# State products of two head pairs moved to the array's other two corners, their sums in a second PSUM bank, first MLP's weights loaded to match

## The chip, the cores and the metric

One core of a Trainium2 chip. The metric is the device time of one execution in microseconds (us); smaller is better. Times are medians of several executions; the profile is one execution, taken by the hardware profiler. Engines are called PE (TensorE matmul), PEld (its weight loads), DVE (VectorE), ACT (ScalarE), POOL (GpSimd) and SP (SyncE, which here only issues DMAs).

## The reference

Attention with decay ("retention") over 2 batches, 8 heads, 768 tokens and 64 channels a head, then two MLPs over the 1536 tokens with 512 channels and 2048 hidden units.

```python
for b in range(nb):                       # blocks of the sequence
    intra = (q_b @ k_b.T * Dmask) @ v_b
    inter = (q_b * lam_pow) @ kv_state
    out[b] = intra + inter
    kv_state = lam_block * kv_state + (k_b * rev_pow).T @ v_b
x = out as (1536, 512)
x = leaky(x @ w_in) @ w_out               # first MLP, slope alpha per hidden unit
x = relu(x @ w2_in)**2 @ w2_out           # second MLP
```

Everything is float32; the weights arrive as 64-bit numbers and are converted on the chip.

## The kernel before

**Retention.** The kernel takes blocks of 128 tokens. Step n of 12 is block c = n // 2 of batch b = n % 2, so the two batches alternate, and the state that step n needs was made by step n - 2. The heads form four pairs a = 0 to 3; of a pair, head t = 0 has its 64 channels in partitions 0 to 63 and head t = 1 in 64 to 127. One step of the main loop is, on PE in this order:

- `outputs(n)`: 8 products of masked scores and v (L1035; stationary 128 x 64), and for c > 0 on top of them, in the same PSUM tile, 8 products of state and q (L1043). The state product of head t uses rows 64t to 64t + 63 of the array and writes to partitions 64t to 64t + 63. So it uses two of the array's four 64 x 64 corners, (0, 0) and (1, 1).
- `products(n)`, called at the end of `outputs(n)` for c < 5: 8 products of the decayed k (called r) and v (L1058), which give the state's increment pk.
- `scores(n + 3)`: 8 products of k and q (L998).

A product in float32 is two PE instructions, so 8 products stand as x16 in the trace.

The order on the other engines is the order in which the loop issues. In step n DVE multiplies the scores of step n + 2 by the decay mask (`decay`, L1010), adds the state (`keep_state`, L1084) and, for the steps without a second copy, takes the rest of the output (`keep_rest`, L1078). ACT copies the output to the first MLP's input in a reduced type (`keep_output`, L1068), makes a second copy `whole` in steps 3, 5, 7 and 9 (L1071) and makes the decayed old state (L1090). POOL makes the factors of step n + 2 (`factors`: q times growth, L1017, then r times fade, L1020) and for steps 3, 5, 7 and 9 the rest of the output from `whole` (L1078). SP issues the loads: k and q of step n + 4 (L897, L898), v and r of step n + 2 (L903, L907), and in eight of the steps one 512 KB piece of the first MLP's weights (`load_piece`, L173). Between these, DVE and ACT convert weight pieces (`Conversion`: L185 and L188 on ACT, L194 and L200 on DVE, the cast L210 on ACT, the rest L216 on DVE); piece number 3 begins in step 9 with L194.

PSUM has 8 banks of 2 KB a partition: four for scores (pool `psc`), two for outputs (`pso`, one bank a step, two in turn) and two for pk (`psk`).

**First MLP.** When the loop is done, PE computes three hidden blocks (`first`, L297, 12 matmuls each) before the first sums (`second`, L358). Step s = 0 to 11 of this stage activates the hidden block on ACT and DVE (L311, L313, L319), splits it into two parts (`cast`, L330 on ACT; `rest`, L338 on DVE), and `second(0)` needs both parts of the block s = 0: its third matmul is the first to read the second part. The remaining hidden units of this MLP and the second MLP follow as Strassen products (L630, L784, L837); their weights are loaded by SP (L391), two 512 KB loads a piece, and converted (L402 on ACT is the first operation on a loaded piece).

The channels of x stand in four blocks of 128 partitions, one for each head pair.

Of the kernel before, what the change touches and what calls it, by code (L numbers as in the profile page):

```python
# [127 lines left out]
def retention_then_two_mlps(  # L128
# [36 lines left out]
    raws, bits, weights = {}, {}, {}  # L165
    loaded = []

    def load_piece(queue=nc.scalar):
        if len(loaded) < len(SEQ):
            j = SEQ[len(loaded)]  # L170
            raws[j] = mem.claim(LOW, RAW + 4 * (len(loaded) % 4), 4)
            loaded.append(j)
            queue.dma_start(raws[j].view(U32), w1[j])  # L173

    class Conversion:
        def __init__(self):
# [208 lines left out]
    def convert(k):  # L385

        half = k % 2
        layer, _, p = pieces[k]
        raw = yield from taken(LOW, RAW + 8 * half, 8)
        for e in range(2):  # L390
            nc.sync.dma_start(  # L391
                raw.view(U32)[:, 2 * e * DM : 2 * (e + 1) * DM],
                (w1, w2)[layer][2 * (2 * p + e) + half],
            )
        bit = yield from taken(LOW, BIT + 7 * half, 4 if half else 7)
        both = raw.view(U32, 2)
        low, high = both[:, :, 0], both[:, :, 1]
        f = bit.view(F32)[:, 0 : 2 * DM]
        x = bit.view(U32)[:, 0 : 2 * DM]
        t = yield from step(  # L400
            ACT, 1.15, now[PE] + LOAD,
            lambda: nc.scalar.activation(  # L402
                f, high.bitcast(F32), AF.Prelu, scale=REBIAS, alpha=SIGN
            ),
        )
        t_low = yield from step(
            ACT, 1.15, t,
            lambda: nc.scalar.activation(low.bitcast(I32), low, AF.Copy, scale=2.0**-29),
        )
# [12 lines left out]
        for i in range(4 if half else 2):  # L422
            m = 2 if half else 7
            done.append((yield from taken(at[2 * half], at[2 * half + 1] + m * i, m)))
        if half:
            cuts = [(f[:, e * DM : (e + 1) * DM], done[e].ap, done[2 + e].ap) for e in range(2)]
            costs = (0.6, 0.7), (0.6, 0.7)
        else:
            a = bit.view(F32)
            cuts = [(a[:, c], done[0].ap[:, c], done[1].ap[:, c])  # L430
                    for c in (slice(0, 2 * DM), slice(2 * DM, None))]
            costs = (1.15, 1.25), (0.85, 0.95)
            a11, a12, a21, a22, s1, s2, s4 = (
                a[:, i * DM // 2 : (i + 1) * DM // 2] for i in range(7)
            )
# [15 lines left out]
        bit.free()  # L451
        pairs[pieces[k]] = done
        made_at[pieces[k]] = now[DVE]
# [424 lines left out]

    psc = actx.enter_context(tc.tile_pool(name="psc", bufs=2, space=PSUM))
    pso = actx.enter_context(tc.tile_pool(name="pso", bufs=2, space=PSUM))  # L880
    psk = actx.enter_context(tc.tile_pool(name="psk", bufs=2, space=PSUM))

# [28 lines left out]
    warm = ap1.tile([128, CH], F32, name="warm")  # L911
    nc.gpsimd.memset(warm, 0.0)

    def keep_warm(i):
        pw = pso.tile([128, NPAIR, CH], F32, tag="o", name=f"warm_ps{i}")
        for a in range(WARM[i]):
            nc.tensor.matmul(pw[:, a % NPAIR, :], warm, warm, start=True, stop=True)

    def where(name, shape, pattern, base, fill, channel=1):

# [48 lines left out]
    fade = ap1.tile([128, H, 1], F32, name="fade")  # L969

    def growth():
        pg = psk.tile([128, 2, NPAIR, D], F32, tag="pk", name="pg")
        pg = pg.rearrange("p a b c -> p (a b c)").rearrange("p (a i) -> p a i", i=CH)
        for a in range(NPAIR):
            nc.tensor.matmul(
                pg[:, a], head[:, a].rearrange("h t d -> h (t d)"), z[:, CH:ZW], start=True,
                stop=True,
            )
        nc.vector.tensor_copy(grow, pg)
        pf = pso.tile([128, NPAIR, CH], F32, tag="o", name="pf")[:, 0, 0:H]  # L980
        nc.tensor.matmul(pf, z[:, CH - 1 : ZW - 1], eye, start=True, stop=True)
        nc.vector.tensor_copy(fade[:, :, 0], pf)

# [42 lines left out]
    def outputs(n):  # L1026
# [1 line left out]
        q_t = qk_t.pop(n)[0]  # L1028
        v_t = vk_t[n][0]
        sc = sc_t.pop(n)[0]  # L1030
        po = pso.tile([128, NPAIR, CH], F32, tag="o", name=f"o{n}")

        for a in range(NPAIR):
            for t in range(2):
                nc.tensor.matmul(  # L1035
                    po[t * D : (t + 1) * D, a, :], v_t[:, 2 * a + t, :], sc[:, t, a, :],
                    start=a == 0, stop=c == 0, skip_group_check=True,
                )
        if c > 0:
            for a in range(NPAIR):  # L1040
                for t in range(2):
                    d = slice(t * D, (t + 1) * D)
                    nc.tensor.matmul(  # L1043
                        po[d, a, :], state[b, c % 2][d, a, :], q_t[d, a, :], start=False,
                        stop=True, skip_group_check=True,
                    )
        if c < NCH - 1 and n not in pk_t:
            products(n)
        vk_t.pop(n)
        return po, pk_t.pop(n, None)  # L1050

    def products(n):
        v_t, r_t = vk_t[n]
        pk_t[n] = pk = psk.tile([128, 2, NPAIR, D], F32, tag="pk", name=f"pk{n}")[:, 0]
        for a in range(NPAIR):
            for t in range(2):
                h = 2 * a + t
# [4 lines left out]

    whole_t = {}

    def keep_output(n, po):
        ti, cols = n // CPT, slice((n % CPT) * CH, (n % CPT + 1) * CH)
        xh = xt[ti][0].view(F32R, TT)
        nc.scalar.copy(xh[:, :, cols], po)  # L1068
        if EARLY_UNITS[n]:
            whole_t[n] = whole = ap2.tile([128, NPAIR, CH], F32, tag="whole", name=f"whole{n}")  # L1070
            nc.scalar.copy(whole, po)  # L1071

    def keep_rest(n, po):

        ti, cols = n // CPT, slice((n % CPT) * CH, (n % CPT + 1) * CH)
        xh, xl = xt[ti][0].view(F32, TT), xt[ti][1].view(F32R, TT)
        engine, full = (nc.gpsimd, whole_t.pop(n)) if n in whole_t else (nc.vector, po)
        engine.tensor_tensor(xl[:, :, cols], full, xh[:, :, cols], ALU.subtract)  # L1078

    def keep_state(n, pk):  # L1080
        c, b = ORDER[n]
# [206 lines left out]
```

## Time and profile before

| | |
|---|---|
| runs | 561.76, 562.46, 564.66 us; median 562.46 |
| profiled execution | 562.17 us, of which the span of the program is 560.4 us |
| PE busy | 554.4 us (99%) |
| DVE, ACT, POOL busy | 370.2, 318.6, 91.7 us |
| granted PE clock | full in all of the 40 slices |
| DMA | 93.1 MB |

The span starts with the first instruction. A row of a timeline gives start, duration, engine, line of the kernel, operation, written tile <- read tiles, shapes, count, and in brackets the idle time before it with what ended it. A window gives the busy time of each engine in a stretch. Matmuls overlap their successors, so the cost of a group of matmuls is read from its start to the start of the next group.

### The profile page before, as it was taken

To read this page: it belongs to the slowest core of one execution; us is meant where nothing else is said; L and a number is where in the kernel's file an instruction comes from. 1 tells how busy PE (TensorE), PEld (TensorE's weight loads), DVE (VectorE), ACT (ScalarE), POOL (GpSimd) and SP (SyncE) were. 2 spreads that over 40 slices of the span, in tenths; PEclk is the share of its full clock that TensorE was granted. 3 is DMA by queue.
4 is the path that set the end of the run, shared out by engine and by line. 5 is a ranking of instruction groups with operands and counts; after the bars stand their busy time and mean duration, and the time that the engine had idled before them with its cause. 6 is when DMAs were issued, how large, how long until landed. Compare 5 with 4: busy or idle time off the path is not lost.

```text
span 560.4 us, 8645 instructions
## 1 busy us (share of the span) xinstructions
PE 554.4 (99%) x3376; PEld 499.5 (89%) x3376; DVE 370.2 (66%) x539; ACT 318.6 (57%) x509; POOL 91.7 (16%) x122
## 2 busy tenths in 40 slices
PE   8999999999999999999999999999999999999997
PEld 8888888899999999999999988898988899899896
DVE  3887987867867687554788767876668733333225
ACT  2675886868775665655667656755655622341220
POOL 2798240001310000430003500000000001400000
PEclk9999999999999999999999999999999999999999
DMA  7995987827771213996223985251032001933003
GB/s 250 392 390 187 340 320 275 308 96 246 140 180 76 76 75 116 370 286 149 76 97 61 342 280 216 76 175 67 30 143 77 1 1 56 330 126 108 1 0 112
DMA packets 39992, 93.11 MB, mean 166 GB/s; under 512 B 4232, under 2 KB 13712, under 8 KB 39952
## 3 DMA queue, kind: packets, MB, share of 16 engines
q1 hardware_dynamic: 27136, 60.98, 30.5%
q0 software_dynamic: 12672, 31.46, 20.1%
q8 instruction: 26, 0.43, 0.3%
q10 hardware_dynamic: 144, 0.13, 0.1%
q14 instruction: 14, 0.11, 0.1%
HBM read 64.23 MB, written 25.96 MB: 161 GB/s over the span
## 4 chain that ended last, share of the span: by engine, by line
PE 95%; DMA 3%; DVE 1%; SPq 0%; issue 0%; DVEq 0%
PE p L630 37%; PE acc L837 24%; PE acc L784 12%; PE acc1n L784 6%; PE h L297 6%; PE acc L358 6%; PE o L1043 2%; PE o L1035 2%; PE s L998 1%; DMA q<-in_qt_dram 1%; DMA r<-in_kr_dram 1%; PE pk L1058 1%; DMA zd<-z 1%; DMA lam_sb<-in_lam_dram 0%; DVE err L957 0%; PE last L837 0%
## 5 line engine op out<-in xcount | busy, mean ns | idle before, releaser
L630 PE MATMUL p<-high_r_mem,low_r_mem 128*128 128x384 f32 x840 | 162.4, 335 | 0.0
L630 PEld LDWEIGHTS p<-high_r_mem,low_r_mem 128*128 128x128 f32 x840 | 148.5, 188 | 8.1
L837 PE MATMUL acc<-low_r_mem 128*128 128x512 f32 (+1 forms) x576 | 144.4, 392 | 0.0
L837 PEld LDWEIGHTS acc<-low_r_mem 128*128 128x128 f32 x576 | 106.7, 188 | 18.2
L678 DVE TENSOR_TENSOR low_r_mem<-high_mem,low_r_mem 128x768 fp32r<-128x768 f32 x56 | 53.6, 958 | 34.1 <-ACT low_r_mem L674 33.1
L784 PE MATMUL acc<-low_r_mem 128*128 128x512 f32 x288 | 74.4, 394 | 0.0
L662 DVE SCALAR_TENSOR_TENSOR high_mem<-p,high_mem 128x384 f32<-128x384 f32 x56 | 31.2, 557 | 59.3 <-ACT high_mem L653 35.0
L630 PE MATMUL p<-high_r_mem 128*128 128x384 f32 x336 | 65.0, 335 | 0.0
L653 ACT ACTIVATE high_mem<-p 128x384 f32<-128x384 f32 x56 | 27.6, 492 | 61.7 <-PE p L630 61.7
L630 PEld LDWEIGHTS p<-high_r_mem 128*128 128x128 f32 x336 | 59.5, 188 | 3.3
L784 PEld LDWEIGHTS acc<-low_r_mem 128*128 128x128 f32 x288 | 53.3, 188 | 8.3
L674 ACT CAST low_r_mem<-high_mem 128x768 fp32r<-128x768 f32 x56 | 46.8, 836 | 18.4 <-DVE high_mem L662 13.8
L722 DVE TENSOR_TENSOR high_mem<-p,high_mem 128x384 f32<-128x384 f32 x28 | 15.6, 557 | 58.0 <-PE p L630 51.7
L470 POOL DMA_DIRECT2D high_r_mem<-parts x28 | 15.0, 546 | 225.5 <-ACT p L691 150.1
L449 DVE TENSOR_TENSOR low_r_mem<-low_mem,low_r_mem 128x512 fp32r<-128x512 f32 (+2 forms) x48 | 39.6, 850 | 0.8 <-ACT low_r_mem L445 0.7
L445 ACT CAST low_r_mem<-low_mem 128x512 fp32r<-128x512 f32 (+2 forms) x48 | 34.7, 752 | 3.8 <-DVE low_mem L417 2.6
L784 PE MATMUL acc1n<-low_r_mem 128*128 128x256 f32 x288 | 36.4, 282 | 0.0
L784 PEld LDWEIGHTS acc1n<-low_r_mem 128*128 128x128 f32 x288 | 35.9, 191 | 0.0
L417 DVE CUSTOM_DVE_ANT_0 low_mem<-low_mem 128x2048 uint16<-128x2048 uint16 x28 | 34.2, 1221 | 1.6 <-issue 0.5
L358 PE MATMUL acc<-low_r_mem 128*128 128x512 f32 x144 | 35.2, 390 | 0.0
L701 ACT COPY high_mem<-p 128x384 f32<-128x384 f32 x28 | 13.5, 482 | 37.9 <-PE p L630 37.9
L297 PE MATMUL h<-low_r_mem 128*128 128x512 f32 x144 | 34.4, 390 | 0.0
(95 smaller groups left out, 661.7 us busy)
## 6 DMA issues: line engine op xcount, KB each, us to landing
low_mem<-in_w_dram SPq DMA_DIRECT2D x64, 512.0 KB, 4.3
parts<-high_r_mem POOLq DMA_DIRECT2D x28, 384.0 KB, 7.2
high_r_mem<-parts POOLq DMA_DIRECT2D x28, 384.0 KB, 5.9
sums<-high_mem SPq DMA_DIRECT2D x18, 256.0 KB, 4.5
sums<-high_mem POOLq DMA_DIRECT2D x18, 256.0 KB, 6.2
k<-in_kt_dram SPq DMA_DIRECT2D x12, 256.0 KB, 5.9
q<-in_qt_dram SPq DMA_DIRECT2D x12, 256.0 KB, 5.2
v<-in_vr_dram SPq DMA_DIRECT2D x12, 256.0 KB, 5.8
```

What stands on the lines that cost most here:

```text
L297: nc.tensor.matmul(ph, w[:, cols], x[:, c, :], start=c == 0 and i == 0, stop=c == NC - 1 and i == 2)
L358: nc.tensor.matmul(acc[t][i], w[:, cols], g, start=f == part[0] and j == 0, stop=f == part[-1] and j == 2,)
L417: lambda: nc.vector.tensor_tensor(n, n, low.bitcast(I32), ALU.add),
L445: ends_at.append((yield from step(ACT, us, t, lambda: nc.scalar.copy(hi, y))))
L449: lambda: nc.vector.tensor_tensor(lo, y, hi.bitcast(F32), ALU.subtract),
L630: nc.tensor.matmul(ps, w[:, cols], x[:, c, :], start=start and c == 0 and j == 0, stop=c == 1 and j == 2, skip_group_check=True,)
L653: ACT, 0.5, now[PE], lambda: nc.scalar.activation(out, ps, AF.Relu, scale=scale)
L662: lambda: nc.vector.scalar_tensor_tensor(out, ps, 0.0, out, ALU.max, op),
L674: t = main(ACT, 0.85, g_at[k], lambda: nc.scalar.copy(hi, x))
L678: lambda: nc.vector.tensor_tensor(lo, x, hi.bitcast(F32), ALU.subtract),
L784: nc.tensor.matmul(ps, w[:, rows], g[:, e, cols], start=start and e == 0 and j == 0, stop=n in ends and e == 1 and j == 2, skip_group_chec ...
L837: nc.tensor.matmul(ps, g[:, e, rows], w[:, cols], start=(n in begins or cut > 0) and e == 0 and i == 0, stop=n in ends and e == 1 and i == ...
```

## The change

The state products of pairs 2 and 3 swap halves in the output: head t writes to partitions 64(1 - t) on, so that they use the corners (0, 1) and (1, 0). They and their masked-score products write to a second bank. Each step now has one PSUM tile of two banks (`out_bank`): for c > 0 pairs 0 and 1 stand in the first half of bank 0, pairs 2 and 3 in the first half of bank 1, and pk in the second half of bank 1; for c = 0 the four pairs stand in bank 0 as before. The pool `psk` is gone. For 0 < c < 5 `products(n)` is issued ahead of the masked-score products, not behind the state products. The order of the state products is 0, 2, 1, 3. ACT and DVE read the outputs from two banks in one instruction.

In x the channel blocks 2 and 3 now have their partition halves exchanged. The first MLP's input weights are loaded to match: each such 512 KB load is three DMAs (blocks 0 and 1 on all partitions; blocks 2 and 3 in two crosswise halves of 64 partitions). This touches four of the eight loads of L173 (steps 0, 2, 4 and 8) and twelve of the 56 of L391.

```diff
+    def load_rows(queue, to, of, swapped):
+        if not swapped:
+            queue.dma_start(to, of)
+            return
+        queue.dma_start(to[:, 0:DM], of[:, 0:DM])
+        queue.dma_start(to[0:D, DM : 2 * DM], of[D : 2 * D, DM : 2 * DM])
+        queue.dma_start(to[D : 2 * D, DM : 2 * DM], of[0:D, DM : 2 * DM])
...
-            queue.dma_start(raws[j].view(U32), w1[j])
+            load_rows(queue, raws[j].view(U32), w1[j], j % 2 == 0)
...
-    psk = actx.enter_context(tc.tile_pool(name="psk", bufs=2, space=PSUM))
...
+            out_t[n] = pso.tile([128, 2, NPAIR, CH], F32, tag="o", name=f"o{n}")
...
-        po = pso.tile([128, NPAIR, CH], F32, tag="o", name=f"o{n}")
+        bank = out_bank(n)
+        if c == 0:
+            po = bank[:, 0].rearrange("p (g s) t -> p g s t", g=2)
+        else:
+            po = bank[:, :, 0:2]
+            if c < NCH - 1:
+                products(n)
+
+        def half(a, t):
+            t ^= a // 2
+            return slice(t * D, (t + 1) * D)
...
-                    po[t * D : (t + 1) * D, a, :], v_t[:, 2 * a + t, :], sc[:, t, a, :],
-                    start=a == 0, stop=c == 0, skip_group_check=True,
+                    po[half(a, t), a // 2, a % 2, :], v_t[:, 2 * a + t, :], sc[:, t, a, :],
+                    start=a == 0 or a == 2 and c == NCH - 1, stop=c == 0, skip_group_check=True,
...
-            for a in range(NPAIR):
+            for a in (0, 2, 1, 3):
...
-                        po[d, a, :], state[b, c % 2][d, a, :], q_t[d, a, :], start=False,
-                        stop=True, skip_group_check=True,
+                        po[half(a, t), a // 2, a % 2, :], state[b, c % 2][d, a, :], q_t[d, a, :],
+                        start=False, stop=True, skip_group_check=True,
...
-        if c < NCH - 1 and n not in pk_t:
+        elif n not in pk_t:
             products(n)
...
-        pk_t[n] = pk = psk.tile([128, 2, NPAIR, D], F32, tag="pk", name=f"pk{n}")[:, 0]
+        bank = out_bank(n)[:, 1, 2:4].rearrange("p a i -> p (a i)")
+        pk_t[n] = pk = bank.rearrange("p (a d) -> p a d", d=D)
```

The loads of L391 get the same call, swapped where the piece is an input weight of the first MLP; the warm-up products and the two small products of `growth` write into the same new tiles.

## Rows read from the trace of the kernel before

**Rows 1.** The page, part 1: busy us (share of the span) and instructions by engine.
```profile
PE 554.4 (99%) x3376; PEld 499.5 (89%) x3376; DVE 370.2 (66%) x539; ACT 318.6 (57%) x509; POOL 91.7 (16%) x122
```

**Rows 2.** Windows: busy us by engine, then granted clock, DMA share, GB/s.
```profile
19.00:46.00 27.00, 26.64 (x456) 22.87 (x458) 21.86 (x28) 18.53 (x48) 22.65 (x18) 1.00 1.04 390
46.00:52.20 6.20, 6.20 (x111) 5.17 (x105) 4.22 (x6) 1.93 (x4) 5.08 (x5) 1.00 0.15 58
52.20:61.00 8.80, 8.80 (x41) 7.29 (x40) 8.71 (x17) 8.09 (x15) 6.83 (x10) 1.00 1.15 283
```

**Rows 3.** Timeline of PE: a warm-up, steps 8 to 10, the first MLP's start.
```profile
12.76 2.05 PE L917 MATMUL warm_ps<-warm 128*128 128x128 f32 x16
...
43.88 0.69 PE L1058 MATMUL pk<-v,r 128*64 128x64 f32 x16
44.49 1.16 PE L998 MATMUL s<-q,k 64*128 64x128 f32 x16
45.58 1.09 PE L1035 MATMUL o<-sc,v 128*64 128x128 f32 x16
46.61 1.09 PE L1043 MATMUL o<-q,state 64*64 64x128 f32 x16
47.63 0.69 PE L1058 MATMUL pk<-v,r 128*64 128x64 f32 x16
48.14 1.05 PE L1035 MATMUL o<-sc,v 128*64 128x128 f32 x16
49.12 1.09 PE L1043 MATMUL o<-q,state 64*64 64x128 f32 x16
...
52.18 8.46 PE L297 MATMUL h<-low_r_mem 128*128 128x512 f32 x36
60.48 2.88 PE L358 MATMUL acc<-low_r_mem 128*128 128x512 f32 x12
```

**Rows 4.** Timeline of POOL: r of steps 6, 8 and 9, q of 10 and 11, the rest of step 9.
```profile
34.09 1.49 POOL L1020 TENSOR_TENSOR r<-r,fade 128x512 f32<-128x512 f32 x1
...
40.69 1.27 POOL L1020 TENSOR_TENSOR r<-r,fade 128x512 f32<-128x512 f32 x1
...
44.31 1.04 POOL L1020 TENSOR_TENSOR r<-r,fade 128x512 f32<-128x512 f32 x1 [0.67 <-DMA r<-in_kr_dram]
...
46.55 2.51 POOL L1017 TENSOR_TENSOR q<-q,grow 128x512 f32<-128x512 f32 x2
49.01 1.73 POOL L1078 TENSOR_TENSOR low_r_mem<-whole,low_r_mem 128x512 fp32r<-128x512 f32 x1
```

**Rows 5.** Timelines of ACT and DVE: step 9, and the split of the first hidden block.
```profile
47.74 0.59 ACT L1068 CAST low_r_mem<-o 128x512 fp32r<-128x512 f32 x1 [1.47 <-PE o L1043]
48.23 0.59 ACT L1071 COPY whole<-o 128x512 f32<-128x512 f32 x1
...
48.36 0.43 DVE L1084 TENSOR_TENSOR state<-pk,old 128x256 f32<-128x256 f32 x1 [1.44 <-PE pk L1058]
...
49.53 1.49 DVE L194 TENSOR_SCALAR low_mem<-low_mem 128x512 uint32<-128x512 uint32 x1
...
54.16 0.42 DVE L194 TENSOR_SCALAR low_mem<-low_mem 128x512 uint32<-128x512 uint32 x1
...
59.63 0.68 DVE L338 TENSOR_TENSOR low_r_mem<-high_mem,low_r_mem 128x512 fp32r<-128x512 f32 x1
```

**Rows 6.** DMA issues (KB each, us to landing): r from 14 to 46 us, weights over all.
```profile
r<-in_kr_dram SPq DMA_DIRECT2D x7, 256.0 KB, 5.9
...
low_mem<-in_w_dram SPq DMA_DIRECT2D x64, 512.0 KB, 4.3
```

**Rows 7.** Loads of L391 issued from 84 to 99 us, and what first reads the earlier pair.
```profile
L391 SPq DMA_DIRECT2D low_mem<-in_w_dram x4: 327/732/1260, 86.5 to 97.0; - x4
...
DMA to landing us min/median/max: 7.9/8.3/8.8
...
101.97 1.15 ACT L402 ACTIVATE low_mem<-low_mem 128x1024 f32<-128x1024 f32 x1
```

More of the change, by code (lines that the diff above doesn't have):

```diff
@@ L390, in convert @@
         for e in range(2):
-            nc.sync.dma_start(
-                raw.view(U32)[:, 2 * e * DM : 2 * (e + 1) * DM],
-                (w1, w2)[layer][2 * (2 * p + e) + half],
+            load_rows(
+                nc.sync, raw.view(U32)[:, 2 * e * DM : 2 * (e + 1) * DM],
+                (w1, w2)[layer][2 * (2 * p + e) + half], layer == 0 and half == 0,
             )
@@ L912, in retention_then_two_mlps, with out_bank @@
     nc.gpsimd.memset(warm, 0.0)
+    out_t = {}
+    def out_bank(n):
+        if n not in out_t:
+            out_t[n] = pso.tile([128, 2, NPAIR, CH], F32, tag="o", name=f"o{n}")
+        return out_t[n]
     def keep_warm(i):
-        pw = pso.tile([128, NPAIR, CH], F32, tag="o", name=f"warm_ps{i}")
+        pw = out_bank(0)
         for a in range(WARM[i]):
-            nc.tensor.matmul(pw[:, a % NPAIR, :], warm, warm, start=True, stop=True)
+            nc.tensor.matmul(pw[:, 0, a % NPAIR, :], warm, warm, start=True, stop=True)
     def where(name, shape, pattern, base, fill, channel=1):
@@ L971, in growth @@
     def growth():
-        pg = psk.tile([128, 2, NPAIR, D], F32, tag="pk", name="pg")
-        pg = pg.rearrange("p a b c -> p (a b c)").rearrange("p (a i) -> p a i", i=CH)
+        bank = out_bank(1)
+        pg = bank[:, 0]
         for a in range(NPAIR):
@@ L979, in growth @@
         nc.vector.tensor_copy(grow, pg)
-        pf = pso.tile([128, NPAIR, CH], F32, tag="o", name="pf")[:, 0, 0:H]
+        pf = bank[:, 1, 0, 0:H]
         nc.tensor.matmul(pf, z[:, CH - 1 : ZW - 1], eye, start=True, stop=True)
@@ L1043, in outputs @@
                     nc.tensor.matmul(
-                        po[d, a, :], state[b, c % 2][d, a, :], q_t[d, a, :], start=False,
-                        stop=True, skip_group_check=True,
+                        po[half(a, t), a // 2, a % 2, :], state[b, c % 2][d, a, :], q_t[d, a, :],
+                        start=False, stop=True, skip_group_check=True,
                     )
-        if c < NCH - 1 and n not in pk_t:
+        elif n not in pk_t:
             products(n)
         vk_t.pop(n)
+        out_t.pop(n)
         return po, pk_t.pop(n, None)
@@ L1063, in retention_then_two_mlps, with x_view @@
     whole_t = {}
+    def x_view(i, dtype, n):
+        cols = slice((n % CPT) * CH, (n % CPT + 1) * CH)
+        x = xt[n // CPT][i].view(dtype, TT).rearrange("p (g s) t -> p g s t", g=2)
+        return x[:, :, :, cols]
     def keep_output(n, po):
-        ti, cols = n // CPT, slice((n % CPT) * CH, (n % CPT + 1) * CH)
-        xh = xt[ti][0].view(F32R, TT)
-        nc.scalar.copy(xh[:, :, cols], po)
+        nc.scalar.copy(x_view(0, F32R, n), po)
         if EARLY_UNITS[n]:
-            whole_t[n] = whole = ap2.tile([128, NPAIR, CH], F32, tag="whole", name=f"whole{n}")
-            nc.scalar.copy(whole, po)
+            whole = ap2.tile([128, NPAIR, CH], F32, tag="whole", name=f"whole{n}")
+            whole_t[n] = whole.rearrange("p (g s) t -> p g s t", g=2)
+            nc.scalar.copy(whole_t[n], po)
     def keep_rest(n, po):
-        ti, cols = n // CPT, slice((n % CPT) * CH, (n % CPT + 1) * CH)
-        xh, xl = xt[ti][0].view(F32, TT), xt[ti][1].view(F32R, TT)
         engine, full = (nc.gpsimd, whole_t.pop(n)) if n in whole_t else (nc.vector, po)
-        engine.tensor_tensor(xl[:, :, cols], full, xh[:, :, cols], ALU.subtract)
+        engine.tensor_tensor(x_view(1, F32R, n), full, x_view(0, F32, n), ALU.subtract)
     def keep_state(n, pk):
```

## The prediction

> **What bounds the kernel now.** The page comes first: PE is busy 99% of the span and no other engine over 66% [rows 1]. Read alone, that says that every microsecond taken from PE is a microsecond of the run. The retention stage, where the change works, ends at 52.18 us, so I cut windows there [rows 2]. From 19 to 46 us PE is busy 26.64 of 27.00 us, but the DMA engines are full as well (share 1.04, 390 GB/s) and POOL is busy 22.65. From 46 us on the DMA engines are nearly idle (0.15) and PE has no gap. From 52.2 to 61 us, behind the change, DVE is busy 8.71 of 8.80 us and ACT 8.09. So PE is one of several full resources, and each stretch has another one beside it. Then the timelines: PE for the price of each group [rows 3], POOL for what PE would wait for [rows 4], ACT and DVE for the handover to the first MLP [rows 5], the DMA issues for the loads [rows 6, 7].
>
> **State products.** Sixteen instructions of a state group go two at a time; the next group starts 1.02 us later (46.61 to 47.63). Sixteen full-array warm-ups of the same 128 columns go one at a time and take 2.05 us, the state group 1.09 [rows 3]. Eight array steps fewer are worth 0.96 us, 0.12 each. Four at a time is four steps instead of eight: 0.48 us off, 0.54 left. Bounds: 0 (they do not run four at a time) and 0.51 (half of 1.02). I take 0.48, because two at a time already gave its whole share. Ten steps have such a group.
>
> **Products first.** pk now stands beside the masked-score group, which has the same 128 x 64 stationary. That neighbourhood exists once, in steps 9 and 10: pk to the next group is 0.51 there (47.63 to 48.14) against 0.61 before scores (43.88 to 44.49) [rows 3]. 0.10 off in eight steps. On PE alone the change is worth 10 x 0.48 + 8 x 0.10 = 5.6 us. A step costs 1.09 (scores) + 0.51 + 1.03 (masked scores, 45.58 to 46.61) + 0.54 = 3.17 us, before 3.75.
>
> **The wait it adds.** pk needs r, and r is POOL's last product of a step. Before, PE asked for it 2.05 us after the step's start; now it asks first, and everything of the step is queued behind. r ends at 35.58 for step 6, 41.96 for step 8 and 45.35 for step 9 [rows 4]. Before, these steps started at 34.33, 41.83 and 45.58 (45.58 less multiples of 3.75). Carried on with 3.17: step 6 starts at 35.58, step 7 at 38.75, step 8 at max(41.92, 41.96) = 41.96, step 9 at max(45.13, 45.35) = 45.35. Nothing that PE gains before step 9 survives; of all of it 0.23 us are left. r of step 9 itself waited 0.67 us for its load [rows 4], and that load stands in the full DMA queue, which does not go faster because PE does.
>
> **The end of the stage.** From 45.35: pk 0.51, masked scores 1.03, state 0.54, so step 9 ends at 47.43. Step 10: 0.98 (48.14 to 49.12 [rows 3]) and 0.54, to 48.95. q of steps 10 and 11 is ready by 49.06 [rows 4], in time for both. Step 11 writes the tile of step 9, and must wait for that tile's readers, now also for the state add on DVE, since pk lives there.
>
> When can that add read? Before, it started at 48.36, in the middle of ACT's two copies of the same step (47.74 to 48.82) [rows 5], out of another bank. Now pk shares a bank with outputs that ACT is copying. Either the add keeps its place right behind the products (47.6), or it comes behind both copies. I take the later. ACT starts 0.11 after the group's end as before, at 47.54; its second copy starts 0.49 later and takes 0.59, to 48.62; the add takes 0.43, to 49.05. With 0.1 for the handover step 11 starts at 49.15 and ends 1.03 + 0.54 later: the first MLP starts on PE at 50.72, against 52.18 [rows 3]. 1.46 us gained so far. The Trainium skill (PSUM — Partial Sum Buffer, "PSUM bank collisions raise a hardware error") says that two engines must not be on one bank and quadrant at the same time, reads against reads included. By that rule the add waits for both copies, which is the value taken; without it, step 11 would start at 48.95, 0.2 us earlier, and the next part would come out otherwise.
>
> **What takes the next part of it.** PE reaches `second(0)` 8.30 us after the MLP's start [rows 3]: now at 59.02, its third matmul (2.88 / 12 = 0.24 each) at 59.50, before at 60.96. That matmul reads what L338 on DVE finishes at 60.31 [rows 5]. L338 ends a dense chain of ACT and DVE work [rows 2] that begins with L194 in step 9. L194 took 1.49 us there and 0.42 later [rows 5]: it ended 0.28 us after POOL's subtraction for step 9 (49.01 to 50.74 [rows 4]), which it ran beside. After the change the add starts at 48.62, L194 1.17 us behind as before, at 49.79, still inside that subtraction, which follows q and r and so the load. So L194 ends at 51.02 as before, and the chain does not move. PE then waits at the third matmul until 60.31 + 0.1: 0.55 us ahead of before. Bounds: 0.3 (r 0.2 late, POOL and the chain with it) to 1.46 (the chain moves along). I take 0.55. Behind this point ACT and DVE have room again, and PE carries the gain to the end.
>
> **Costed at nothing.** Eight more DMA issues in the retention stage, 0.33 us each [rows 7], 2.6 us on SP. Loads of 256 KB take 5.9 us to land there while the weights' 512 KB take 4.3 over the whole run [rows 6]: the loads wait in the DMA engines, not for SP, and bytes and their order stay. Were the engines to run dry, r of step 9 and the end would slip by as much. Of the MLP's loads twelve become three: 24 more issues, 1.3 us for a pair. The tightest of the six pairs lands by 86.88 + 8.8 = 95.7 and is first read at 101.97 [rows 6, 7], so 6.3 us cover it; without that cover each late pair would cost up to 1.3 us. The copies out of two banks have the same elements; I allow 0.05 us each way for a copy, which ACT has room for before step 9. Steps 0 and 1 and the small products keep their place.
>
> **Sum.** 562.17 (the profiled execution: span 560.4 and 1.8 around it) less 0.55 is 561.6. That execution lies 0.3 under the median of the three runs, so I put the number at 561.7.
>
> **Rivals.**
> The PE-only sum: all 5.6 us arrive, 556.6. For it stands PE at 99%. Against it, r is late for the new place in steps 6, 8 and 9 and POOL idles for a load [rows 4] with DMA full [rows 2]. It would need loads that land some 4 us earlier. Chance 0.05.
>
> The chain moves along: the state add comes right behind the products, L194 finds POOL in q's product instead, and DVE and ACT are some 2 us ahead when the MLP starts. Then 1.5 us arrive, 560.6. Chance 0.22.
>
> The corners do not overlap: state groups stay at 1.02. This is the change not doing what it says. A step is 3.65; step 6 still starts at 35.58, step 9 at 35.58 + 3 x 3.65 = 46.53, and with 0.51 + 1.03 + 1.02 and twice (0.98 + 1.02) and 0.02 the MLP starts at 53.1, 0.9 us later than before: 563.1. It decides as soon as r of step 6, not PE, sets the phase. Against it: the two corners used so far do overlap [rows 3]. Chance 0.13.
>
> The crosswise halves are slow, the slower side: if a 64-partition load runs at half rate, three such loads ahead of r of step 9 (steps 0, 2, 4) with 256 KB in halves each, 0.79 MB, take 4.0 instead of 2.0 us at 390 GB/s [rows 2]. r, POOL's subtraction and the chain slip by 2.0 us; L338 ends at 62.3, PE goes on 1.4 us later than before: 563.6. It decides once the loss is over 0.55 us. No row has a 64-partition load. The Trainium skill (DMA: Bandwidth & Descriptors, "Rules for kernel authors") says that two transfers to disjoint partition halves share the same engines and bring nothing over one of 128 partitions; by that, bytes count as before and this price would be 0. No row here shows it. Chance 0.08.
>
> **How the numbers follow.** The forecast, 0.3 to 0.9 us gained, has 0.52; rivals as above. A measurement of this kernel can tell about 0.5%, 2.8 us, from no change. Only the PE-only sum passes that on the fast side; I give 0.08 with its partial forms. Slower by that needs more than either slow rival gives: 0.05, for halves much slower than half rate or a late conversion. No change: 0.87. The range goes from 560.2 (the moved chain less 0.4 of scatter) to 563.3 (no overlap, with a little scatter); it leaves out the PE-only sum and most of the slow halves.
>
> **What the next profile would show.** State groups followed after about 0.54 us instead of 1.02. PE waiting on POOL r at the head of steps 2 to 9, step 9 starting near 45.4. L1084 starting behind L1071 in step 9. The first L297 near 50.7, then a gap of 0.8 us in the first L358. The forecast is wrong if step 9 starts well before 45, if the L358 group follows without a gap, or if in_w loads delay r.

## The result, and the profile after

| | before | after |
|---|---|---|
| median of 9 runs each, taken side by side | 562.74 us | 565.98 us (564.56 to 567.95) |
| profiled execution (span) | 562.17 us (560.4) | 566.53 us (564.7) |

The ratio is 1.0056, with an interval from 1.0044 to 1.0069: slower by 3.2 us, where 0.8 us of gain on the median was forecast and 563.3 was the upper end of the range. The change does what it says and takes work from PE all the same. The page of the kernel after, part 1, answers to [rows 1]:

```profile
PE 551.7 (98%) x3376; PEld 496.1 (88%) x3376; DVE 369.7 (65%) x539; ACT 318.7 (56%) x509; POOL 90.1 (16%) x122
```

PE has 2.7 us less to do and the span is 4.3 us longer, so PE now waits for 7 us more. The windows of the kernel after (columns as in [rows 2]) say where:

```profile
19.00:46.00 27.00, 20.25 (x374) 16.66 (x374) 17.76 (x23) 15.32 (x42) 17.70 (x15) 0.94 1.02 317
46.00:52.20 6.20, 5.93 (x120) 5.04 (x124) 5.04 (x7) 4.42 (x10) 5.00 (x5) 1.00 1.06 317
52.20:61.00 8.80, 8.77 (x102) 6.99 (x97) 7.03 (x10) 5.58 (x11) 8.15 (x10) 1.00 0.58 171
61.00:84.00 23.00, 22.73 (x101) 18.49 (x100) 21.41 (x35) 18.30 (x30) 6.62 (x13) 1.00 1.05 321
```

From 19 to 46 us PE is busy 20.25 us in place of 26.64, and so are DVE, ACT and POOL less busy than in [rows 2]: the whole stage waits for something. The DMA engines are as full as before (1.02), but they move 317 GB/s in place of 390. And where they were nearly idle before, from 46 to 52.2 us (0.15), they are now still full. The same bytes take longer.

The timeline of PE in the kernel after, against [rows 3] (L1084 is pk, L1012 the scores, L1059 the masked scores, L1067 the state products, L305 and L366 the first MLP's `first` and `second`):

```profile
22.75 0.67 PE L1067 MATMUL o<-q,state 64*64 64x128 f32 x16
23.34 1.16 PE L1012 MATMUL s<-q,k 64*128 64x128 f32 x16
...
33.73 0.69 PE L1084 MATMUL o<-v,r 128*64 128x64 f32 x16 [1.28 <-POOL r L1034]
39.04 0.69 PE L1084 MATMUL o<-v,r 128*64 128x64 f32 x16 [2.06 <-POOL r L1034]
...
50.52 0.69 PE L1084 MATMUL o<-v,r 128*64 128x64 f32 x16 [0.23 <-POOL r L1034]
51.03 1.04 PE L1059 MATMUL o<-sc,v 128*64 128x128 f32 x16
52.01 0.67 PE L1067 MATMUL o<-q,state 64*64 64x128 f32 x16
...
55.95 8.47 PE L305 MATMUL h<-low_r_mem 128*128 128x512 f32 x36
64.25 0.62 PE L366 MATMUL acc<-low_r_mem 128*128 128x512 f32 x2
65.14 2.56 PE L366 MATMUL acc<-low_r_mem 128*128 128x512 f32 x10 [0.27 <-DVE low_r_mem L346]
```

A state group takes 0.59 us to the next group (22.75 to 23.34) in place of 1.02, so the corners do overlap. But pk, now at the head of a step, waits for POOL's r in steps 2 to 6 and 9, for 6.7 us in all. Step 9 starts at 50.52, not at 45.58, and the first MLP at 55.95, not at 52.18. The timeline of POOL, against [rows 4], names what r waits for:

```profile
37.73 1.25 POOL L1034 TENSOR_TENSOR r<-r,fade 128x512 f32<-128x512 f32 x1 [0.91 <-DMA r<-in_kr_dram]
...
41.80 1.04 POOL L1034 TENSOR_TENSOR r<-r,fade 128x512 f32<-128x512 f32 x1 [1.59 <-DMA r<-in_kr_dram]
...
49.42 1.04 POOL L1034 TENSOR_TENSOR r<-r,fade 128x512 f32<-128x512 f32 x1 [1.20 <-DMA r<-in_kr_dram]
```

The last row is r of step 9: it ends at 50.46 and was waiting for its load, as in [rows 4], only 5.1 us later (45.35 before). The lower rate is enough for that: from 19 us to the landing of this load at 44.31, the kernel before moves 25.3 us x 390 GB/s = 9.9 MB, which at 317 GB/s take 31 us, to about 50; the load lands at 49.42. Then ACT and DVE in step 9 and at the split of the first hidden block, against [rows 5] (L1097 and L1101 are ACT's two copies, L1112 the state add, L202 what was L194, L346 what was L338):

```profile
52.74 0.59 ACT L1097 CAST low_r_mem<-o 128x512 fp32r<-128x512 f32 x1 [1.17 <-PE o L1067]
53.22 0.59 ACT L1101 COPY whole<-o 128x512 f32<-128x512 f32 x1
...
53.85 0.42 DVE L1112 TENSOR_TENSOR state<-o,old 128x256 f32<-128x256 f32 x1 [1.81 <-ACT whole L1101]
...
55.87 0.41 DVE L202 TENSOR_SCALAR low_mem<-low_mem 128x512 uint32<-128x512 uint32 x1
...
64.41 0.68 DVE L346 TENSOR_TENSOR low_r_mem<-high_mem,low_r_mem 128x512 fp32r<-128x512 f32 x1
```

The add stands behind both copies, and DVE's chain from its start to the end of L346 takes 11.2 us (12.0 before), all of it some 5 us later. What differs in the loads is seen in the DMA issues of the kernel after, against [rows 6]; 16 of the 64 weight loads are now three DMAs:

```profile
low_mem<-in_w_dram SPq DMA_DIRECT2D x48, 512.0 KB, 4.3
...
low_mem<-in_w_dram SPq DMA_DIRECT2D x16, 256.0 KB, 6.3
low_mem<-in_w_dram SPq DMA_DIRECT2D x32, 128.0 KB, 6.0
```

### The profile page after: what moved, and what is told of

It reads as the page before. It is cut to its first block, busy times and chain, and to the rows that moved or that the text cites. A ratio compares the mean times of both kernels' runs of the same rounds, so it can differ in the third digit from the quotient of the medians.

```text
span 564.7 us, 8690 instructions
## 1 busy us (share of the span) xinstructions
PE 551.7 (98%) x3376; PEld 496.1 (88%) x3376; DVE 369.7 (65%) x539; ACT 318.7 (56%) x509; POOL 90.1 (16%) x122
## 4 chain that ended last, share of the span: by engine, by line
PE 88%; DVE 1%; issue 0%
PE p L638 36%; PE acc L845 23%; PE acc L792 12%; PE acc1n L792 6%; PE acc L366 6%; PE h L305 4%; DVE high_mem L532 1%; PE last L845 0%; DVE low_r_mem L346 0%; DVE low_mem L208 0%; DVE high_mem L327 0%; DVE low_r_mem L224 0%; DVE low_mem L866 0%; DVE low_mem L202 0%
## 5 line engine op out<-in xcount | busy, mean ns | idle before, releaser
L366 PE MATMUL acc<-low_r_mem 128*128 128x512 f32 x144 | 35.5, 391 | 0.3 <-DVE low_r_mem L346 0.3
L305 PE MATMUL h<-low_r_mem 128*128 128x512 f32 x144 | 34.4, 390 | 0.0
```

Source lines behind the costliest of these rows:

```text
L305: nc.tensor.matmul(ph, w[:, cols], x[:, c, :], start=c == 0 and i == 0, stop=c == NC - 1 and i == 2)
L366: nc.tensor.matmul(acc[t][i], w[:, cols], g, start=f == part[0] and j == 0, stop=f == part[-1] and j == 2,)
```

## The experiments

The theory, H in the expectations: loads of 64 partitions make the full DMA engines move less, so r comes late, and all else of the change does as predicted. Its rivals: it is the crossing of the rows that costs (X; e2); it is the number of DMAs (C; e3); it is pk at the head of the step, in a bank that ACT reads, which ties PE to r and to ACT, the late loads being a consequence (O; e1, e4, e5, e12).

The ratios below are to runs of the kernel before on the same chip, 562.4 to 562.5 us by the median (562.74 for the kernel after). One table carries most of the readings. "r(9)" is when POOL ends r of step 9, "MLP" when PE starts the first MLP, "third" the start of the third matmul of `second(0)`. Where no wait stands ahead of that matmul it is taken as two twelfths of the group behind the group's start, as in the prediction.

| kernel | r(9) | MLP | third | profiled | profiled less third | median |
|---|---|---|---|---|---|---|
| before | 45.35 | 52.18 | 60.96 | 562.17 | 501.2 | 562.5 |
| after | 50.46 | 55.95 | 65.14 | 566.53 | 501.4 | 565.98 |
| e1 plain loads | 45.08 | 51.07 | 60.27 | 561.67 | 501.4 | 561.37 |
| e2 halves, not crossed | 50.69 | 56.18 | 65.37 | 566.73 | 501.4 | 566.41 |
| e3 three full DMAs | 46.06 | 51.80 | 61.00 | 562.42 | 501.4 | 563.62 |
| e4 before, crosswise loads | 49.09 | 55.02 | 63.83 | 565.17 | 501.3 | 564.99 |
| e5 plain, pk last | 44.69 | 49.43 | 59.20 | 560.55 | 501.4 | 561.44 |
| e6 plain, pk in the middle | 44.26 | 49.36 | 58.77 | 560.15 | 501.4 | 561.24 |
| e7 plain, old corners | 45.51 | 53.00 | 61.82 | 563.01 | 501.2 | 563.36 |
| e8 crosswise in the MLP only | 45.06 | 51.03 | 60.23 | 561.58 | 501.4 | 561.57 |
| e9 even and odd partitions | 48.36 | 53.85 | 63.05 | 577.33 | 514.3 | 577.17 |
| e10 plain, state add first | 45.49 | 53.09 | 61.90 | 563.09 | 501.2 | 563.63 |
| e12 crosswise, pk last | 48.84 | 53.57 | 63.35 | 564.78 | 501.4 | 565.26 |
| e13 v in halves | 54.72 | 60.21 | 69.41 | 570.52 | 501.1 | 569.28 |

In the profiled executions of twelve of the thirteen changed kernels, and of the kernel before, what follows the third matmul takes 501.1 to 501.4 us. So, but for e9, the time of a profiled execution is settled by then; nothing later gives back or takes.

**e1: the change with plain loads.** The rows of the weights' blocks 2 and 3 are exchanged in memory, before the launch, so that each load can be one DMA again. On the chip only the loads differ from the kernel after.

```diff
-        queue.dma_start(to[:, 0:DM], of[:, 0:DM])
-        queue.dma_start(to[0:D, DM : 2 * DM], of[D : 2 * D, DM : 2 * DM])
-        queue.dma_start(to[D : 2 * D, DM : 2 * DM], of[0:D, DM : 2 * DM])
+        queue.dma_start(to, of)
...
-        a = w_in.reshape(NC, 128, NF, 128).transpose(2, 1, 0, 3).reshape(NF, 1, 128, DM)
+        a = w_in.reshape(NC, 2, D, NF, 128).copy()
+        if swap:
+            a[2:] = a[2:, ::-1]
+        a = a.reshape(NC, 128, NF, 128).transpose(2, 1, 0, 3).reshape(NF, 1, 128, DM)
```

> The changed kernel with the exchanged rows put in place when the weights are laid out in memory, so that each load is one DMA of 128 partitions again; all else as changed. Theory H (loads of 64 partitions are slow and delay r): DMA back to about 390 GB/s from 19 to 46 us, r of step 9 done near 45.4, first L305 at 50.7 to 51.3, 561.2 to 562.4 us. Theory C (three DMAs in place of one hold up SP) and theory X (the crossing) say the same here. Theory O (pk ahead of the other products makes PE wait, whatever the loads do): 564 us or more, with r late in most steps.

Measured: 561.37 us (560.87 to 562.79), ratio 0.9982 [0.9973, 0.999]. The whole loss is gone and a small gain is left. The window of e1:

```profile
19.00:46.00 27.00, 24.24 (x486) 20.45 (x482) 21.23 (x29) 19.17 (x51) 23.12 (x19) 1.00 1.03 387
```

With the order, the corners and the banks of the change, the DMA engines move 387 GB/s again. So the loads are not late because of the order. The timeline of PE in e1 is the one that the prediction worked out (its L1082 is pk, L1057 the masked scores, L1065 the state products, L303 and L364 the MLP):

```profile
45.63 0.69 PE L1082 MATMUL o<-v,r 128*64 128x64 f32 x16
46.15 1.04 PE L1057 MATMUL o<-sc,v 128*64 128x128 f32 x16
47.12 0.67 PE L1065 MATMUL o<-q,state 64*64 64x128 f32 x16
47.72 1.09 PE L1057 MATMUL o<-sc,v 128*64 128x128 f32 x16
...
51.07 8.50 PE L303 MATMUL h<-low_r_mem 128*128 128x512 f32 x36
59.40 0.61 PE L364 MATMUL acc<-low_r_mem 128*128 128x512 f32 x2
60.27 2.58 PE L364 MATMUL acc<-low_r_mem 128*128 128x512 f32 x10 [0.25 <-DVE low_r_mem L344]
```

**e2: halves, but not crossed.** The memory layout of e1, the three DMAs of the change, each half going to its own partitions.

```diff
-        queue.dma_start(to[0:D, DM : 2 * DM], of[D : 2 * D, DM : 2 * DM])
-        queue.dma_start(to[D : 2 * D, DM : 2 * DM], of[0:D, DM : 2 * DM])
+        queue.dma_start(to[0:D, DM : 2 * DM], of[0:D, DM : 2 * DM])
+        queue.dma_start(to[D : 2 * D, DM : 2 * DM], of[D : 2 * D, DM : 2 * DM])
```

> As the plain loads, but blocks 2 and 3 come in two DMAs of 64 partitions each that do not cross (rows 0 to 63 to partitions 0 to 63). Theory H: as slow as the change, 565 to 567 us, about 320 GB/s at a full DMA share. Theory C: as slow as the change too. Theory X: as fast as the plain loads.

Measured: 566.41 us (564.93 to 568.24), ratio 1.0071 [1.0046, 1.0095], as slow as the change. That the rows cross is not what costs. The window of e2:

```profile
19.00:46.00 27.00, 22.00 (x408) 18.55 (x404) 18.73 (x24) 17.07 (x47) 18.29 (x16) 0.94 1.01 325
```

**e3: three DMAs of all partitions.** As e2, with blocks 2 and 3 split by columns instead of by partitions.

```diff
-        queue.dma_start(to[0:D, DM : 2 * DM], of[0:D, DM : 2 * DM])
-        queue.dma_start(to[D : 2 * D, DM : 2 * DM], of[D : 2 * D, DM : 2 * DM])
+        queue.dma_start(to[:, DM : DM + DM // 2], of[:, DM : DM + DM // 2])
+        queue.dma_start(to[:, DM + DM // 2 : 2 * DM], of[:, DM + DM // 2 : 2 * DM])
```

> As the plain loads, but each of these loads is three DMAs of 128 partitions (256, 128 and 128 KB, split by columns). Theory H: as fast as the plain loads, 561 to 562.7 us, with at most 0.3 us for smaller packets. Theory C: as slow as the change, 565 to 567 us. Theory X: as fast as the plain loads.

Measured: 563.62 us (562.42 to 564.19), ratio 1.0016 [1.0007, 1.0025], with this window:

```profile
19.00:46.00 27.00, 22.41 (x447) 18.76 (x446) 19.51 (x26) 17.86 (x49) 21.57 (x17) 1.00 1.03 366
```

Between e1 and e2, in bandwidth (366 of 387 and 325 GB/s) as in time. Of the 5.0 us from e1 to e2, 2.2 come with the three DMAs and 2.8 more with the halves, by the medians. That is above what H gave: the halves are only the larger part, and cutting a load into three costs by itself. But e3 also shortens rows: two of its three parts bring 1 KB to a partition, where the parts of e2 bring 2 KB, and no run tells what the short rows cost of the 2.2 us. The profiled execution, 562.42 us, is the fastest of its ten runs; by its row in the table the three DMAs cost 0.7 us.

**e4: the loads of the change in the kernel before.** Order, corners and banks of before; memory rows exchanged beforehand, so that the crosswise loads put them straight.

```diff
-            queue.dma_start(raws[j].view(U32), w1[j])
+            load_rows(queue, raws[j].view(U32), w1[j], j % 2 == 0)
```

> The kernel before with the change's crosswise loads alone (rows exchanged beforehand in memory, so that the crossing puts them back). Theory H: r late here too, but PE asks for it 2 us later in a step, so 563.5 to 566 us, with DMA near 320 GB/s in the retention stage. Theory O: no change against the kernel before, 562.7 us.

Measured: 564.99 us (564.16 to 565.56), ratio 1.0044 [1.003, 1.0058], 330 GB/s from 19 to 46 us, and in POOL's timeline r of step 9:

```profile
48.05 1.04 POOL L1028 TENSOR_TENSOR r<-r,fade 128x512 f32<-128x512 f32 x1 [0.43 <-DMA r<-in_kr_dram]
```

The loads alone cost the old kernel 2.5 us; so theory O, which had no change here, fails. It is hurt less than the change, which loses 4.6 us from e1 to after. Of these, about 1 us is the gain that the old kernel does not have to lose (e5 against before), and 0.7 go with pk at the head of the step (e12): with crosswise loads and pk last, old and new kernel are 0.3 us apart (564.99 and 565.26).

**e8: crosswise in the MLP's loads only.** As the kernel after, except that the four loads of the retention stage are plain (their rows exchanged in memory) and the twelve of L391 stay three DMAs each.

```diff
-            load_rows(queue, raws[j].view(U32), w1[j], j % 2 == 0)
+            load_rows(queue, raws[j].view(U32), w1[j], False)
```

> The changed kernel with its crosswise loads only in the twelve loads for the Strassen part; the four loads in the retention stage are single DMAs (their rows put in place beforehand). If the cost arises only where the DMA engines are full and r is awaited: as fast as all plain loads, 561.0 to 561.9 us. If the later loads cost something as well: 562.3 us or more.

Measured: 561.57 us (560.92 to 562.63), ratio 0.9988 [0.9979, 0.9997], e1's within the scatter. The whole cost lies in four loads of the retention stage, of which three stand ahead of r of step 9. The 24 further DMAs of the twelve MLP loads cost nothing: from 61 to 250 us, where they are issued, PE is busy without a gap in e8 as in e1, and the DMA share of e8 is 0.93, 0.72 and 0.58 (61 to 84, 84 to 140 and 140 to 250 us).

**e13: another load in halves.** A dose test: e1, with v of every step in two DMAs of 64 partitions.

```diff
-        nc.sync.dma_start(v_t, vr[n])
+        for t in range(2):
+            nc.sync.dma_start(v_t[t * D : (t + 1) * D], vr[n][t * D : (t + 1) * D])
```

> Plain weight loads, but each v load (256 KB) comes in two DMAs of 64 partitions. A dose test of theory H: eight such loads are ahead of r of step 9, against three in the change, so the window from 19 to 46 us moves at 300 GB/s or less at a full share, r of step 9 ends after 55, 570 us or more. If only the weight loads are slow in halves: 561.4 to 563 us.

Measured: 569.28 us (568.04 and 570.52, two runs), ratio 1.0121 [1.0099, 1.0143]. The window of e13, and r of step 9 in its POOL timeline:

```profile
19.00:46.00 27.00, 20.98 (x384) 17.54 (x382) 17.91 (x22) 16.25 (x46) 17.31 (x15) 0.94 1.01 295
```

```profile
53.68 1.04 POOL L1033 TENSOR_TENSOR r<-r,fade 128x512 f32<-128x512 f32 x1 [2.82 <-DMA r<-in_kr_dram]
```

A little less than expected, but in the sense that H gave: with other data, and no weight load cut, loads of 64 partitions lower the rate of the full engines (295 GB/s) and delay r, by 9.6 us against e1. That each v load is now two DMAs is part of this too, and not separated.

**e9: even and odd partitions.** As e1, with blocks 2 and 3 in two DMAs of 64 partitions each, every second partition instead of a contiguous half.

```diff
-        queue.dma_start(to, of)
+        queue.dma_start(to[:, 0:DM], of[:, 0:DM])
+        queue.dma_start(to[0:128:2, DM : 2 * DM], of[0:128:2, DM : 2 * DM])
+        queue.dma_start(to[1:128:2, DM : 2 * DM], of[1:128:2, DM : 2 * DM])
```

> Rows in place beforehand; blocks 2 and 3 come in two DMAs of 64 partitions each, the even ones and the odd ones, so both spread over all 128 partitions. If loads of 64 partitions are slow because all of a DMA's rows lie in one half of the partitions (theory H1): as fast as three DMAs of 128 partitions or faster, 561.5 to 563.8 us, DMA at 360 GB/s or more from 19 to 46 us. If they are slow because a DMA has 64 rows only (theory H2): as slow as the uncrossed halves, 565 to 568 us, near 325 GB/s.

Measured: 577.17 us, ratio 1.0271 [1.0252, 1.029], with this window:

```profile
19.00:46.00 27.00, 21.73 (x434) 18.23 (x432) 17.63 (x26) 17.12 (x47) 20.53 (x17) 1.00 0.98 341
```

The time and the rate decide nothing. In two of the four loads SP issues the first of the three parts (29.29 and 41.51) and the next only 2.7 and 3.5 us later, and the stages behind the third matmul take 13 us more than in every other version. This form of load has a cost of its own. What was asked is seen in the packets, below under the step that failed: they are not slowed as in e2, which speaks for H1.

**e5, e6: pk last, pk in the middle, with plain loads.** e1 with `products(n)` behind the state products, and between the masked scores and the state products. The diff of e6 (the start flags follow the order in both):

```diff
             po = bank[:, :, 0:2]
-            if c < NCH - 1:
-                products(n)
...
+        if c < NCH - 1 and n not in pk_t:
+            products(n)
         if c > 0:
...
-        elif n not in pk_t:
-            products(n)
```

> Plain loads, with pk issued behind the state products as before (still in the second bank). If PE's early wait for r costs the end nothing more than the prediction says, because the chain of ACT and DVE work sets the first sums: 561.0 to 561.8 us, as with pk first, with the stage ending up to 1.3 us earlier and a longer wait in the first L364 group. If the order itself costs: under 560.7 us.

> Plain loads, with pk issued between the masked-score products and the state products, so that PE asks for r 1.0 us later and still saves the change of tiling. If the ACT and DVE chain sets the first sums: the stage ends 0.3 to 1.3 us earlier than with pk first, the wait in the first L364 group grows, 560.8 to 561.7 us. If r's place costs by itself: 560.6 us or less.

Measured: e5 561.44 us (560.41 to 562.54), ratio 0.9982 [0.9974, 0.9991]; e6 561.24 us (560.15 to 562.56), ratio 0.9979 [0.9969, 0.999]. By the medians neither differs from e1. In the profiled executions the third matmul stands at 59.20 and 58.77 against 60.27, 1.1 and 1.5 us sooner, and their total is sooner by as much; but both stand at the low end of their runs (e6's is the lowest of its twelve). Whether the middle place is worth something is not settled by these runs. It is at least no loss, and e6 has the best median of all versions. In each of the three the third matmul waits for DVE's second part of the hidden block, so that chain still sets the end, as the prediction had it.

**e7: old corners.** Plain loads, pk first, two banks; the state products of all pairs in the two corners of before, no rows exchanged.

```diff
         def half(a, t):
-            t ^= a // 2
             return slice(t * D, (t + 1) * D)
...
-            for a in (0, 2, 1, 3):
+            for a in (0, 1, 2, 3):
```

> The changed kernel with the state products of all pairs in the two old corners and plain loads without any exchange; two banks and pk first stay. By the prediction's own sum for groups that do not overlap: state groups of 1.02 us, L305 about 53.1, 562.9 to 563.6 us. If the corners are worth nothing because r and the chain set the end: 561.2 to 561.9 us, as with the corners.

Measured: 563.36 us (562.4 to 564.27), ratio 1.0017 [1.0008, 1.0026]. The timeline of PE in e7 (L1064 are the state products):

```profile
47.89 1.09 PE L1064 MATMUL o<-q,state 64*64 64x128 f32 x16
48.91 1.09 PE L1056 MATMUL o<-sc,v 128*64 128x128 f32 x16
...
53.00 8.50 PE L303 MATMUL h<-low_r_mem 128*128 128x512 f32 x36
61.34 2.88 PE L364 MATMUL acc<-low_r_mem 128*128 128x512 f32 x12
```

A state group takes 1.02 us again. The corners are worth 2.0 us by the medians (563.36 less 561.37); without them the rest of the change, pk at the head of the step and the two banks, is a loss of 0.9 us.

**e10: the state add ahead of ACT's copies.** e1, with DVE's add issued before ACT's two copies of the same bank.

```diff
+        if pk is not None:
+            keep_state(n, pk)
         keep_output(n, po)
...
-        if pk is not None:
-            keep_state(n, pk)
```

> Plain loads, and in each step the state add is issued ahead of ACT's copies of the output, so that the copies wait for the add and not the add for the copies. If the chain that starts behind the state add of step 9 is what takes the rest of the gain: the add starts near 47.9, the first shift behind it ends before POOL's subtraction for step 9 runs, the first sums no longer wait, 559.8 to 560.9 us. If the chain hangs on something else: 561.0 to 561.7 us, as with plain loads.

Measured: 563.63 us (562.74 to 564.18), ratio 1.002 [1.0011, 1.0028]; a miss, slower than e1 by 2.3 us. The timeline of PE in e10:

```profile
39.13 0.69 PE L1082 MATMUL o<-v,r 128*64 128x64 f32 x16 [0.75 <-POOL r L1032]
...
43.13 0.69 PE L1082 MATMUL o<-v,r 128*64 128x64 f32 x16 [0.74 <-POOL r L1032]
...
47.13 0.69 PE L1082 MATMUL o<-v,r 128*64 128x64 f32 x16 [0.75 <-issue]
...
51.47 1.09 PE L1057 MATMUL o<-sc,v 128*64 128x128 f32 x16 [0.56 <-ACT whole L1099]
```

The copies now wait for the add, and the add stands behind the decay in DVE's queue. pk stands at 39.13, 43.13 and 47.13 in steps 7 to 9, 4.0 us a step in place of 3.7 and 3.2 in e1. In steps 7 and 8 PE waits for r. In step 9 the trace names nothing, but pk starts 0.1 us behind ACT's second copy out of the tile that it writes to (46.45 to 47.03), and in step 11 the wait is for that copy by name.

**e12: crosswise loads, pk last.** The kernel after with the order of e5 (its loads take the change's three lines in place of e1's one, and nothing is exchanged in memory).

```diff
             po = bank[:, :, 0:2]
-            if c < NCH - 1:
-                products(n)
...
-        elif n not in pk_t:
+        if c < NCH - 1 and n not in pk_t:
             products(n)
```

> The changed kernel with its crosswise loads, and pk issued last as before. If the early asking for r makes the late loads dearer: r of step 9 ends near 50 as in the change, but PE needs it 1.6 us later in the step, 563.8 to 565.3 us. If the place of pk does not matter: 565.5 to 567 us, as the change.

Measured: 565.26 us (564.04 to 565.82, four runs), ratio 1.0047 [1.0033, 1.006]. Near the upper edge of what was expected. With late loads the old place of pk saves 0.7 us by the medians, and the two intervals overlap; most of the loss stays. So the order can make late loads dearer by little, if at all; with plain loads (e1, e5) it makes no difference.

## Why the prediction was wrong, step by step

**The step that failed** is under "Costed at nothing": "the loads wait in the DMA engines, not for SP, and bytes and their order stay". Bytes and order did stay, and by their share the engines were as full as before, but they moved less: 317 GB/s in place of 390 from 19 to 46 us, and r of step 9 came 5.1 us late. The prediction's own sign of being wrong, "if in_w loads delay r", is what came. The DMA engines from 28 to 30 us, kernel after and e1 (packets, MB, share of 16 engines):

```profile
q1 hardware_dynamic: 259, 0.46, 100.4%
```

```profile
q1 hardware_dynamic: 406, 0.74, 98.1%
```

A packet, the many of 2 KB and the few of 4 bytes together, took 16 x 2 us x 1.004 / 259 = 124 ns in the one and 16 x 2 us x 0.981 / 406 = 77 ns in the other, with 1.8 KB in either. This stretch is one of the slowest. From 19 to 46 us, counted from the packets in the traces, a 2 KB packet took 104 ns in the mean in the kernel after and 87 in e1. The median is 84 in both; the difference lies in those that took far longer. Over 100 ns took, of the 2 KB packets,

- 0.5 to 1.4% in before and in the versions with plain loads (e1, e5 to e8, e10),
- 2.7% in e3 and 4.3% in e9,
- 19.5 to 22.4% in after, e2, e4 and e12,
- 42.9% in e13.

So the slow packets come with loads whose 64 rows lie in one half of the partitions, and more of such loads make more of them. Three DMAs in place of one (e3) bring few, and so do 64 rows spread over all partitions (e9). In the kernel after the slow ones are 790 packets, while at most 512 of that stretch can belong to halves (four loads of 128 rows): other loads in flight slow down as well.

The step compared KB per load [rows 6] with a share that was over 1.0 already [rows 2], and took the 390 GB/s that go with it for a fixed rate. It is not: it hangs on the loads that are in flight.

The mechanism was on record as a rival, "The crosswise halves are slow", with its place and its way to the end right: r of step 9, then POOL's subtraction and the chain, then PE. Its size was not. It priced r at 2.0 us later, by half the rate for the bytes in halves alone; measured are 5.1 us (50.46 less 45.35), since other loads that are in flight with them slow down too, and since three DMAs for one load cost something by themselves (e3). From the forecast to the kernel after that makes 65.14 less 60.4 = 4.7 us at the third matmul, where the rival had 2.0.

Beside its chance, 0.08, stood a rule. The Trainium skill (DMA: Bandwidth & Descriptors, "Rules for kernel authors") says that two transfers to disjoint partition halves share the same engines, and to use one transfer of 128 partitions instead. That the halves share the engines agrees with the share of 1.01 in e2. The price of 0 that the prediction read out of it does not: 325 GB/s against 387, 5.0 us. The rule's advice holds here; that bytes then count as before was an inference, and no row of the profile carried it.

**The steps that held** are seen in e1, where only the loads differ:

- State groups: 0.54 us were forecast, 0.60 measured (47.12 to 47.72), so 0.42 off in place of 0.48. The step from two at a time to four does not halve the group as the step from one to two did.
- pk beside the masked scores: 0.51 forecast, 0.52 measured. A step: 3.17 forecast, 3.18 measured from pk of step 8, where PE waited for r, at 42.45 to that of step 9 at 45.63. That r sets the phase held too: steps 6 to 9 were forecast at 35.58, 38.75, 41.96 and 45.35 and start at 35.57, 38.75, 42.45 and 45.63.
- Step 9 to the MLP: 5.37 us forecast (45.35 to 50.72), 5.44 in e1 (45.63 to 51.07) and 5.43 in the kernel after. Only its start was wrong, by the loads.
- The state add comes behind both copies: at 53.85 in the kernel after, 0.04 us behind ACT's second copy. This was the value that the rule on banks in the Trainium skill (PSUM — Partial Sum Buffer, "PSUM bank collisions raise a hardware error") gave, and the trace agrees; e10 shows the same two readers in turn with the roles exchanged. The rival "The chain moves along", which needs the add right behind the products, is not had by reversing them.
- What takes the next part: the timeline of DVE in e1 (L222 is what was L216, L200 what was L194, L344 what was L338):

```profile
48.97 0.43 DVE L1110 TENSOR_TENSOR state<-o,old 128x256 f32<-128x256 f32 x1 [1.51 <-ACT whole L1099]
49.31 1.53 DVE L222 TENSOR_TENSOR low_r_mem<-low_mem,low_r_mem 128x512 fp32r<-128x512 f32 x1
50.76 0.41 DVE L200 TENSOR_SCALAR low_mem<-low_mem 128x512 uint32<-128x512 uint32 x1
...
59.53 0.68 DVE L344 TENSOR_TENSOR low_r_mem<-high_mem,low_r_mem 128x512 fp32r<-128x512 f32 x1
```

  L344 ends at 60.21 (60.31 forecast) and the third matmul starts at 60.27 (60.41). In the profiled executions e1 is 0.50 us ahead of before, where 0.55 were forecast. The cause named for the chain is half right: in e1 the rest ahead of L200 is what is stretched, to 1.53 us beside POOL's subtraction (49.01 to 50.29; the same operation takes 0.69 at 52.59), while L200 takes 0.41. That their end, 51.17, is near the forecast's 51.02 all the same is luck.
- The MLP's 24 further DMAs cost nothing (e8).
- "The corners do not overlap" was worked out as 563.1 with the MLP at 53.1. e7 makes that case: 563.36, and 53.00.

**The clock** explains none of it that these runs show. In the kernel after the granted clock is half of full from 40.3 to 43.7 us (1.2 of 2.4 GHz), after PE had waited 2.06 us for r and gone on at 39.04; the groups there take up to twice as long (scores 2.01 us to the next group, 1.20 one step later). But r of step 9 waits for its load after that and sets the end again, and e4 has its loss with the full clock from 19 to 46 us. Of the nine runs of the kernel after, two kept the full clock throughout, by the mean granted clock: they took 565.47 and 567.95 us.

**What stays open.** Why a packet takes longer when loads to one half of the partitions are in flight. That engines stand idle while others have a queue is not what the traces suggest: from 19 to 46 us 16.5 packets are under way at a time in e1 and 16.2 in e2, and under 12 of them in 0.0 and 4.3% of the time. But the traces do not name the engine of a packet, so an uneven load is not excluded, and no run here tells it from a slower transfer at its destination. e9 is a single form of spread rows with a delay of its own, so that the half of the partitions is what matters is likely, not proven. Open are also: why three full DMAs in place of one cost 2.2 us by the medians (0.7 in the profiled executions), with the rows of 1 KB as one candidate; why e9 is issued late and loses 13 us behind the first sums; and whether pk in the middle is better than pk first.

## What to carry to other kernels

Where the DMA engines are full, their rate is not a constant: a change that keeps every byte but cuts loads into partition halves needs a price; it can't be costed at nothing (here some 5 us at r for three loads). If rows must stand crosswise, exchange them where the data is laid out, and keep each load one DMA over all partitions. And where an engine is at 99%, look at what feeds the first instruction of its step: of 5.6 us of matmul time by the forecast, the best version here brings 1.2 us by the medians, since r and then the chain of ACT and DVE set the end.

## What the runs showed of the hardware that was not expected

- Loads of 64 partitions, with the DMA engines full by their share: 317 to 338 GB/s in after, e2, e4 and e12, 295 in e13, against 386 to 390 in before, e1 and e5 to e8, with loads of 128 (380 in e10). The share of busy time is 1.01 to 1.02 in the first and 1.03 to 1.04 in the second, so the share does not tell the two cases apart; the times of the packets do (2 KB packets over 100 ns: 19.5% or more against 1.4% or less).
- One load as three DMAs of 128 partitions, two of them with rows of 1 KB: 366 GB/s in place of 387 in the same stretch.
- Loads to every second partition (e9): in two of four loads the next DMA was issued 2.7 and 3.5 us later, and the run was 15 us slower than before; but only 4.3% of the 2 KB packets took over 100 ns.
- Sixteen 64 x 64 x 128 products over all four corners, in two banks: 0.60 us; over two corners: 1.02 us.
- PE at half its clock for 3.4 us in the kernel after, soon after a wait of 2.06 us.
